# Second value tile of a local attention: 64 of its 96 rows copied from the first value tile by GpSimd instead of loaded by DMA

## The chip, the core and the metric

The kernel runs on one core of a Trainium2 chip. The metric is the device time of one execution in microseconds (us); three runs of the kernel before have a median of 644.54 us (642.48 to 645.26). The engines are TensorE (PE; its weight loads are listed as PEld), VectorE (DVE), ScalarE (ACT), GpSimd (POOL) and SyncE (SP, which here only issues DMAs). Each works through its own list of instructions in order. Waits between them are semaphores.

## What is computed

A local attention feeds a mixture of experts. Only the attention is touched.

```python
B, H, S, D = 4, 8, 768, 64            # block = 32, window = 16
k_sum = k.reshape(B, H, nb, block, D).max(axis=3)       # 24 block keys
v_sum = v.reshape(B, H, nb, block, D).mean(axis=3)      # 24 block values
scores_l = scale * q @ k.T, masked to |i - j| < 16
scores_s = scale * q @ k_sum.T + log(block)
a = softmax(concat[scores_l, scores_s])
attn = a @ concat[v, v_sum]
# then: noisy top-2 gate over 8 experts, relu(x @ w1) @ w2, weighted sum
```

For 64 queries the mask leaves at most 64 + 2*16 = 96 keys. With the 24 block keys a block of 64 queries thus has 120 keys and 120 value rows.

## The kernel before

**Tiles.** The attention goes through 24 tiles of 128 queries (4 batches of 6 tiles, all 8 heads at once). Tile t = 6*b + j is treated as two blocks of 64 queries (`blk` 0 and 1), each with its own 120 keys in `KX[t % 3]` and its own 120 value rows. The values of block 0 are `VE[b % 2][:, j]`: a tile of 128 rows loaded by `load_ve` (rows P*j to P*j+127 of the padded values `vt`), of which rows 0 to 95 are the local values; rows 96 to 119 are overwritten with the 24 block sums once these are computed. The values of block 1 are `VD[b % 2][j % 3]`: rows 0 to 23 hold the block sums, and `v_load` brings rows P*j+64 to P*j+159 of `vt` into rows 24 to 119. Each row is 8 heads of 65 floats, 520 in all (64 values and a one, which gives the softmax's denominator). Rows 64 to 95 of block 0's tile and the first 32 rows of block 1's are the same values; so are rows 0 to 31 of the next tile's `VE` and the last 32 rows of block 1's.

**Columns of the keys.** `L0 = (0, NB)` says where the 96 local keys stand among the 120: for block 0 at 0 to 95 with the block keys behind, for block 1 the block keys stand in columns 0 to 23 and the local keys behind them.

**The order of the work** is written out by hand in one loop over t from -2 to 22. Iteration t records, in this order: the normalization of tile t-1 on DVE (`norm`, L363 to L369; from the second batch on with `kx_sum(t+3)` on GpSimd inside it); the scores of tile t+2 on PE (`scores`, L318); the row maximum of tile t+2 on DVE (`smax`, L325); the transposes of tile t+1's probabilities on PE (`p_trans`, L341); the mask of tile t+3 (`mask_sums`, L308); the exponentials of tile t+2 on ACT (`sexp`, L333); `kx_local(t+3)`, two GpSimd copies of local keys into `KX` (L124); the transposes of the finished tile t-1 (`x_pe`, L378); the product of probabilities and values of tile t on PE (`av`, L354); then `v_load(t+3)`, one DMA on SP's queue (L290), and `x_out(t-2)`. Other work hangs at fractions of t in a table `todo` (`at`, `run`): key and value loads of the next batch, `v_sums` (block sums of the values on PE, copied out of PSUM, and for batch 0 copied on by six GpSimd copies, L273 and L275, for batch 1 by one, L269), `fill` (GpSimd memsets of 128x1024, L222), the steps of the gate, weight loads.

**The end of the attention.** At t = 20.2, 20.8 and 21.8 GpSimd issues three indirect DMAs (`x_gather(0, 0..2)`, recorded at L90), which gather 128 token rows each for expert 0 into the tiles `xg`. Behind the loop PE transposes two of them (`x_tr`, L835), then does `av(23)`, and then starts expert 0's first matmuls (`mm1`, L854).

**How a dependence is kept.** A copy of GpSimd that reads a value tile waits for its DMA by a semaphore of the DMA (DMAHW for SP's DMAs, DMASW for GpSimd's own); PE waits for GpSimd by a count of its finished instructions. PE, being in order, holds everything behind a matmul that waits.

## Time and profile before

| | |
|---|---|
| median of 3 runs | 644.54 us (642.48 to 645.26) |
| profiled execution, its own time | 642.6 us |
| its span, first to last instruction | 640.8 us, mean granted TensorE clock 0.997 |
| PE / DVE / ACT / POOL busy | 622.5 / 481.3 / 315.9 / 249.0 us |
| attention | roughly the first 130 us of the span |
| DMA traffic | 127.93 MB; `v_load`: 24 DMAs of 195.0 KB, `load_ve`: 24 of 260.0 KB |

The profile is of one execution. "Busy" of PE is modelled from pipelined matmuls. In a timeline row the columns are start and length in us, engine, line of the kernel, operation, output tile <- input tiles, shape, and how many were merged; the brackets tell the idle time before and what ended it. In a row of waits they are who waited for whom, us in total, how often, and the longest. "issue" is idle time for which the profile shows no semaphore.

### The profile page before, as it was taken

How to read it: one execution, taken by the hardware profiler on the slowest of the kernel's cores; microseconds unless marked ns; L12 is line 12 of the kernel's file. 1: busy time of each engine (PE TensorE's matmuls, PEld its weight loads, DVE VectorE, ACT ScalarE, POOL GpSimd, SP SyncE). 2: the span in 40 equal slices, each digit the busy share in tenths (PEclk: the TensorE clock that was granted, in tenths of full speed). 3: DMA queues.
4: the chain of work that ended last, by engine and by line, in shares of the span. 5: the costliest groups of instructions: out<-in, count | busy, mean ns of one | idle time of the engine just before them, and what ended most of it. 6: DMA issues, size and time to landing. Idle time of an engine off the chain costs nothing.

```text
span 640.8 us, 14153 instructions
## 1 busy us (share of the span) xinstructions
PE 622.5 (97%) x5295; PEld 358.8 (56%) x5295; DVE 481.3 (75%) x1039; ACT 315.9 (49%) x692; POOL 249.0 (39%) x432
## 2 busy tenths in 40 slices
PE   8999999999999999999999999999999999999995
PEld 7778777765654544555455544554554455445542
DVE  5768999889796797188868887987898679757410
ACT  4868988941253553075437534654464255425200
POOL 4442224203254324532573266336523532333041
PEclk9999999999999999999999999999999999999998
DMA  9999986788379976547886597759677767763021
GB/s 308 333 292 351 292 266 201 222 318 250 118 217 171 253 186 170 211 122 140 209 265 152 131 228 245 181 133 250 201 189 156 218 205 166 182 198 105 3 96 51
DMA packets 123708, 127.93 MB, mean 200 GB/s; under 512 B 83242, under 2 KB 86674, under 8 KB 123630
## 3 DMA queue, kind: packets, MB, share of 16 engines
q1 hardware_dynamic: 111838, 90.66, 53.3%
q0 software_dynamic: 11792, 36.27, 18.0%
q8 instruction: 44, 0.72, 0.5%
q14 instruction: 34, 0.28, 0.1%
HBM read 81.85 MB, written 25.61 MB: 168 GB/s over the span
## 4 chain that ended last, share of the span: by engine, by line
PE 82%; DVE 6%; issue 3%; DMA 3%; ACT 2%; POOL 1%; SPq 1%; POOLq 0%; DVEq 0%; ACTq 0%
PE pt L1431 29%; PE h L1359 16%; PE h L854 8%; PE pt L909 5%; PE pt L341 3%; PE pt L1359 3%; PE o L1359 3%; PE s L318 3%; PE o L354 3%; PE h L909 2%; DMA xte<-x 2%; PE pt L378 1%; PE o L246 1%; DVE y L920 1%; DVE htl L1394 1%
## 5 line engine op out<-in xcount | busy, mean ns | idle before, releaser
L90 POOL DMA_INDIRECT out_dram<-y,tb x52 | 69.3, 1333 | 169.4 <-DVE y L931 131.6
L90 POOL DMA_INDIRECT xg<-xd,tb x54 | 60.1, 1112 | 118.1 <-DVE dsc L653 32.3
L1431 PEld LDWEIGHTS <-hth 128*128 128x128 f16 x576 | 56.4, 98 | 66.7
L931 DVE SCALAR_TENSOR_TENSOR y<-pt,tb,prev 128x512 f32<-128x512 f32 x42 | 31.5, 750 | 67.4 <-PE pt L1431 49.8
L1359 PEld LDWEIGHTS <-w1h 128*128 128x128 f16 x504 | 48.9, 98 | 38.0 <-issue 4.1
L1431 PE MATMUL pt<-w2h,hth 128*128 128x512 f16 x288 | 69.0, 379 | 0.0
L1431 PE MATMUL pt<-w2h,htl 128*128 128x512 f16 x288 | 69.0, 379 | 0.0
L1431 PE MATMUL pt<-w2l,hth 128*128 128x512 f16 x288 | 69.0, 379 | 0.0
L1359 PEld LDWEIGHTS <-w1l 128*128 128x128 f16 x504 | 49.3, 98 | 34.9
L90 POOL DMA_INDIRECT prev<-out_dram,tb x45 | 52.4, 1165 | 23.7 <-issue 12.8
L333 ACT ACTIVATE p<-s,nm 128x120 f32<-128x120 f32 x192 | 51.0, 376 | 0.8
L854 PE MATMUL h<-xte,w1h 128*128 128x384 f16 (+2 forms) x248 | 48.9, 336 | 1.1 <-DMA xte<-x 1.1
L1431 PEld LDWEIGHTS <-htl 128*128 128x128 f16 x288 | 28.2, 98 | 34.0
L1348 ACT ACTIVATE w1h<-stg 128x768 f16<-128x768 f32 (+1 forms) x24 | 22.7, 944 | 37.9 <-DVE stg L1339 37.9
L1391 ACT ACTIVATE hth<-h 128x384 f16<-128x384 f32 (+4 forms) x48 | 23.8, 496 | 35.6 <-PE h L1359 35.6
L1348 ACT ACTIVATE w1l<-stg 128x768 f16<-128x768 f32 (+1 forms) x24 | 22.5, 942 | 37.2 <-DVE stg L1339 37.2
L1359 PE MATMUL h<-xte,w1h 128*128 128x384 f16 (+4 forms) x180 | 39.7, 329 | 0.7 <-DVE h L1385 0.4
L1359 PE MATMUL h<-xte,w1l 128*128 128x384 f16 (+4 forms) x180 | 39.7, 329 | 0.0
L1339 DVE TENSOR_TENSOR stg<-stg 128x256 f32<-128x256 f32 x96 | 36.2, 419 | 0.8
L854 PEld LDWEIGHTS <-w1h 128*128 128x128 f16 x256 | 24.7, 98 | 20.5 <-issue 2.2
L1312 ACT ACTIVATE x<-xt 128x512 f16<-128x512 f32 (+2 forms) x44 | 26.3, 625 | 19.6 <-issue 17.3
L1394 DVE SCALAR_TENSOR_TENSOR htl<-h,hth 128x384 f16<-128x384 f32 (+4 forms) x48 | 26.3, 562 | 11.8 <-ACT hth L1391 11.5
(301 smaller groups left out, 1292.0 us busy)
## 6 DMA issues: line engine op xcount, KB each, us to landing
stg<-in_w_dram SPq DMA_DIRECT2D x64, 512.0 KB
q<-in_qt_dram SPq DMA_DIRECT2D x24, 256.0 KB
xd<-x SPq DMA_DIRECT2D x24, 256.0 KB
out_dram<-xg SPq DMA_DIRECT2D x8, 768.0 KB
kb<-in_kt_dram SPq DMA_DIRECT2D x6, 768.0 KB
hth<-in_vt_dram SPq DMA_DIRECT2D x12, 260.0 KB
htl<-in_vt_dram SPq DMA_DIRECT2D x16, 195.0 KB
ve<-in_vt_dram SPq DMA_DIRECT2D x12, 260.0 KB
```

The lines of the kernel that those rows point to most:

```text
L90: return nc.gpsimd.indirect_dma_start(**kw)
L333: nc.scalar.activation(PE_[t][:, a, hp, :], SC[t][:, a, hp, :], AF.Exp, bias=NM[t][:, 1, a, hp:hp + 1], scale=0.125)
L854: nc.tensor.matmul(ph[:, :n], w1_of(w, wn, c, f), x[:, xo + c, c0:c1], start=(k == 0), stop=(k == 11))
L909: nc.tensor.matmul(py, hx[:, f, c * P:c * P + P], wv[:, f, :], start=st, stop=sp)
L931: nc.vector.scalar_tensor_tensor(y, py[:, :d], gw, pv[:, :d], op0=OP.mult, op1=OP.add)
L1312: nc.scalar.activation(t[:r, c:c + k], src, AF.Copy)
L1339: nc.vector.tensor_tensor(o, x, y, op=op)
L1348: nc.scalar.activation(hi, x, AF.Copy, scale=W1S)
L1359: nc.tensor.matmul(ph[:, :h], w[:, la, a, P * j:P * j + P], x[:, j, :h], start=start and k == 0, stop=k == 5, skip_group_check=True)
L1391: nc.scalar.activation(hh[:, f, t], src, AF.Relu)
L1394: nc.vector.scalar_tensor_tensor(hl[:, f, t], src, 0.0, hh[:, f, t], op0=OP.max, op1=OP.subtract)
L1431: nc.tensor.matmul(py, x, wv[:, f, :], start=st, stop=sp, skip_group_check=True)
```

## The change

Block 1's value tile gets the layout of block 0's: 96 local rows first, block sums in rows 96 to 119 (`L0 = (0, 0)`, and in `v_sums`, `v_rest` and `kx_sum` the matching places). `v_load` now brings only rows 32 to 63 of the tile (32 rows, 65 KB; for the last tile of a batch rows 32 to 95). A new function `v_copy(t)` lets GpSimd copy rows 0 to 31 from rows 64 to 95 of `VE[:, j]`, and (except in the last tile of a batch) rows 64 to 95 from rows 0 to 31 of `VE[:, j+1]`: 44 copies of 32x520 floats in all. `v_copy(0)` is recorded after the first key copies, `v_copy(t+2)` at the end of iteration t, behind `v_load(t+3)`.

```diff
--- before.py
+++ after.py
@@ -95,7 +95,7 @@
     HWD = 840
     HT = [moe.tile([P, FC, HWD], F16, name=x) for x in ("hth", "htl")]
     KB, KX = [], []
-    L0 = (0, NB)
+    L0 = (0, 0)
     for i in range(2):
         KB.append(keep.tile([P, HP, KW], F32, name=f"kb{i}"))
     for i in range(QN):
@@ -126,8 +126,7 @@
     def kx_sum(t):
         b, j = divmod(t, TS)
         if j < QN:
-            x = KX[t % QN].rearrange("p h b k -> p h (b k)")[:, :, W:W + 2 * NB]
-            (nc.gpsimd if b else nc.vector).tensor_copy(x.rearrange("p h (b n) -> p h b n", b=2),
+            (nc.gpsimd if b else nc.vector).tensor_copy(KX[t % QN][:, :, :, W:W + NB],
                                                         KM[b][:, :, None, :].to_broadcast([P, HP, 2, NB]))
 
     def q_piece(t):
@@ -256,7 +255,7 @@
             for g in range(4):
                 nc.tensor.matmul(pt[32 * g:32 * g + NB, 0:C4], ind[:, j, :], VE[b % 2][:, j, C4 * g:C4 * g + C4],
                                  start=(j == 0), stop=(j == TS - 1), skip_group_check=True)
-        x, y = VE[b % 2][W:W + NB], [z[0:NB] for z in VD[b % 2]]
+        x, y = VE[b % 2][W:W + NB], [z[W:W + NB] for z in VD[b % 2]]
         for g in range(4):
             i, o = pt[32 * g:32 * g + NB, 0:C4], slice(C4 * g, C4 * g + C4)
             if b == 3 and g % 2:
@@ -280,15 +279,23 @@
         nc.sync.dma_start(x[:, j:], x[:, 0, None, :].to_broadcast([NB, TS - j, VB]))
         if b:
             for y in VD[b % 2][b == 1:]:
-                nc.sync.dma_start(y[0:NB], x[:, 0])
+                nc.sync.dma_start(y[W:W + NB], x[:, 0])
 
     VX = {}
 
     def v_load(t):
         b, j = divmod(t, TS)
         y = VD[b % 2][j % 3].rearrange("p (h d) -> p h d", h=H)
-        nc.sync.dma_start(y[NB:NB + VR], vt[b, P * j + 64:P * j + 64 + VR])
+        n = 32 if j < TS - 1 else 64
+        nc.sync.dma_start(y[32:32 + n], vt[b, P * j + 96:P * j + 96 + n])
         VX[t] = [VE[b % 2][:, j].rearrange("p (h d) -> p h d", h=H), y]
+
+    def v_copy(t):
+        b, j = divmod(t, TS)
+        x, y = VE[b % 2], VD[b % 2][j % 3]
+        nc.gpsimd.tensor_copy(y[0:32], x[64:96, j])
+        if j < TS - 1:
+            nc.gpsimd.tensor_copy(y[64:96], x[0:32, j + 1])
 
     SC, PE_, PT, PO, X, XT = {}, {}, {}, {}, {}, {}
 
@@ -1071,6 +1078,7 @@
         if t == -1:
             q_piece(2)
             q_piece(3)
+            v_copy(0)
         run(t + 0.5)
         if t + 2 < NT:
             smax(t + 2)
@@ -1105,6 +1113,8 @@
         run(t + 0.9)
         if 0 <= t and t + 3 < NT:
             v_load(t + 3)
+        if -1 <= t and t + 2 < NT:
+            v_copy(t + 2)
         if t >= 2:
             x_out(t - 2)
 
```

On GpSimd's list, first place: tiles 1 to 4, right after the block sums of batch 0. `htl<-hth` 24x520 and `hth<-hth` 24x520 are the six copies of block sums, `htl<-hth` 32x520 the new copies, `kx_94<-kb_91` is `kx_local(4)`, the keys for the scores of tile 4. Before:

```order
L275 COPY htl<-hth 24x520 [waits DMAHW6_49,DVE_49,Pool_49]
L273 COPY hth<-hth 24x520 [waits DMAHW7_49,PE_49]
L275 COPY htl<-hth 24x520
L273 COPY hth<-hth 24x520 [waits DMAHW0_49,PE_49]
L275 COPY htl<-hth 24x520
L273 COPY hth<-hth 24x520 [waits DMAHW1_49,PE_49]
L124 COPY kx_94<-kb_91 128x4x96 [waits Activation_49,Pool_49]
L124 COPY kx_94<-kb_91 128x4x96 [waits Activation_49]
```

and now:

```order
L274 COPY htl<-hth 24x520 [waits DVE_49]
L272 COPY hth<-hth 24x520 [waits PE_49]
L274 COPY htl<-hth 24x520
L272 COPY hth<-hth 24x520 [waits DMAHW0_49,PE_49]
L274 COPY htl<-hth 24x520
L272 COPY hth<-hth 24x520 [waits DMAHW1_49,PE_49]
L296 COPY htl<-hth 32x520
L298 COPY htl<-hth 32x520
L296 COPY htl<-hth 32x520
L298 COPY htl<-hth 32x520
L124 COPY kx_94<-kb_91 128x4x96 [waits Activation_49,Pool_49]
L124 COPY kx_94<-kb_91 128x4x96 [waits Activation_49]
```

Four copies, `v_copy(1)` and `v_copy(2)`, now stand between the block sums and the keys of tile 4; `v_copy(0)` stands ahead of the block sums.

Second place: the block sums of batch 1 (`vd_102<-ve` 24x520), a memset (`xg`), and the keys of tile 8 (`kx_95`). Before:

```order
L269 COPY vd_102<-ve 24x520 [waits DMAHW6_49,DVE_49,Pool_49]
L222 MEMSET xg_165 128x1024
L130 COPY kx_95<-kmax 128x4x48 [waits PE_49,Pool_49]
L124 COPY kx_95<-kb_92 128x4x96
L124 COPY kx_95<-kb_92 128x4x96 [waits DMAHW1_49]
```

and now:

```order
L268 COPY vd_102<-ve 24x520 [waits DMAHW6_49,DVE_49,Pool_49]
L221 MEMSET xg_165 128x1024 [waits Pool_49]
L296 COPY vd_102<-ve 32x520
L298 COPY vd_102<-ve 32x520 [waits DMAHW7_49,Pool_49]
L129 COPY kx_95<-kmax 128x8x24 [waits PE_49,Pool_49]
L124 COPY kx_95<-kb_92 128x4x96
L124 COPY kx_95<-kb_92 128x4x96 [waits DMAHW1_49]
```

The two copies of `v_copy(6)` stand ahead of the three that fill the keys of tile 8.

Third place: the end of the attention, the three gathers for expert 0 (`DMA xg<-xd`). Before:

```order
L90 DMA xg_165<-xd,tb_181 128x512 [waits DMAHW3_49,DMAHW5_49,DMAHW2_49,DMAHW6_49,DMAHW0_49,DVE_49]
L768 MEMSET tl 128x16
L769 MEMSET side 64x1
L770 MEMSET side 64x1 [waits Pool_49]
L89 MEMSET spacer 1x1
L90 DMA xg_165<-xd,tb_181 128x512
L89 MEMSET spacer 1x1 [waits Pool_49]
L90 DMA xg_166<-xd,tb_181 128x512
L1163 MEMSET hth 128x8x40 [waits DMAHW7_49]
```

and now:

```order
L90 DMA xg_165<-xd,tb_181 128x512 [waits DMAHW5_49,DMAHW6_49,DMAHW2_49,DVE_49]
L775 MEMSET tl 128x16
L776 MEMSET side 64x1
L777 MEMSET side 64x1 [waits Pool_49]
L89 MEMSET spacer 1x1
L90 DMA xg_165<-xd,tb_181 128x512
L296 COPY vd_103<-ve 32x520 [waits DMASW1_49,DMASW0_49,PE_49]
L298 COPY vd_103<-ve 32x520 [waits DMAHW4_49]
L89 MEMSET spacer 1x1 [waits Pool_49]
L90 DMA xg_166<-xd,tb_181 128x512 [waits Pool_49]
L296 COPY htl<-ve 32x520 [waits DMASW2_49,PE_49]
L1173 MEMSET hth 128x8x40 [waits DMAHW7_49,Pool_49]
```

`v_copy(22)` stands between the second and the third gather, with a wait for the landing of the first two (DMASW0, DMASW1), and `v_copy(23)` behind the third, with a wait for its landing (DMASW2). No other engine's order changes; the 24 DMAs of `v_load` keep their places in SP's queue.

## The prediction

> **What bounds the kernel now.** I read the page's first part, then the busy times by stretch, then what PE waited for, then the chain of waits and the timelines at the places that the order of instructions changes.

> ```profile
> span 640.8 us, 14153 instructions
> PE 622.5 (97%) x5295; PEld 358.8 (56%) x5295; DVE 481.3 (75%) x1039; ACT 315.9 (49%) x692; POOL 249.0 (39%) x432
> ...
> 0.00:20.00 20.00, 18.05 (x343) 15.67 (x347) 11.36 (x32) 11.12 (x35) 9.49 (x39) 1.00 0.95 316
> 20.00:60.00 40.00, 37.57 (x796) 29.86 (x789) 29.16 (x73) 32.07 (x104) 15.35 (x33) 1.00 1.00 323
> 60.00:100.00 40.00, 38.72 (x804) 30.78 (x807) 37.52 (x122) 35.69 (x113) 12.40 (x21) 1.00 0.88 275
> 100.00:130.00 30.00, 27.12 (x529) 21.59 (x518) 27.14 (x109) 25.82 (x79) 9.07 (x20) 1.00 0.66 209
> ```

> The four lower rows are stretches of the attention; behind the length stand the busy times of PE, PEld, DVE, ACT and POOL, the granted clock, the DMA engines' share and GB/s. PE is busy nearly all the time, at a granted clock of 1.00; GpSimd is under half busy; the DMA engines are full (1.00) from 20 to 60 us.

> ```profile
> PE pt L341 <- issue: 2.6, 2, 1.4
> ...
> PE h L854 <- DMA xte<-x: 1.1, 1, 1.1
> PE o L354 <- issue: 0.9, 1, 0.9
> ...
> PE s L835 <- DVE xte L825: 0.3, 1, 0.3
> PE pt L854 <- ACT xte L827: 0.2, 1, 0.2
> ```

> So PE sets the end, and its few pauses in the whole execution sum to about 10 us. In the attention not one of the larger ones is a wait for a DMA: the full DMA queues do not hold PE. A change here gains little by moving bytes, and loses whatever it makes PE wait.

> **The change part by part.**

> *Bytes.* 24 DMAs of 195.0 KB become 20 of 65 KB and 4 of 130 KB: 4.68 MB become 1.82 MB. That is 2.9 of 127.93 MB. About half lies in the first 60 us, some 1.4 MB, which at 323 GB/s is 4.4 us of full queues. As PE waits for none of these loads, I count 0. The bound below: the three pauses called "issue" (2.6 + 0.9 = 3.5 us), two of which lie in the full stretch, could be made by the load on the queues and vanish; the bound above is 0.

> *Forty-four copies on GpSimd.*

> ```profile
> L273 POOL COPY hth<-hth 24x520 f32<-24x520 f32 x3 | 1.9, 619 | 0.2
> L275 POOL COPY htl<-hth 24x520 f32<-24x520 f32 x3 | 1.8, 615 | 6.2 <-issue 6.1
> ```

> These copies of 520 floats a row are the nearest rows: 615 ns where the rows move to other partitions (96 on to 0 on, L275), 619 ns where they stay, so the move is free; 32 partitions instead of 24 I take as free too, since every partition has the same 520 elements. 44 * 0.615 = 27 us on an engine with 46 us of work in the 130 us. On the average that fits. But GpSimd also makes the keys for which PE waits, in order, and what counts is what stands behind the copies.

> *First place: the keys of tile 4.*

> ```profile
> 17.54 0.61 POOL L275 COPY htl<-hth 24x520 f32<-24x520 f32 x1 [6.08 <-issue]
> ...
> 20.89 0.62 POOL L273 COPY hth<-hth 24x520 f32<-24x520 f32 x1
> 21.57 2.74 POOL L124 COPY kx<-kb 128x384 f32<-128x384 f32 x6
> ...
> 22.41 1.08 PE o L354 x32
> 23.50 0.98 PE s L318 x32
> 24.48 1.15 PE pt L341 x8
> ```

> Six copies of block sums start 0.67 us apart ((20.89 - 17.54) / 5) and end at 21.51; then come the keys of tiles 4 to 6, 0.46 us each (2.74 / 6), so tile 4's two are ready at 22.5, 1.0 us before the scores of tile 4 start on PE (23.50). Now `v_copy(1)` and `v_copy(2)` stand between. `v_copy(1)` ends at 21.57 + 0.67 + 0.62 = 22.86, and `av(1)`, which reads that tile, would start at 22.41: 0.45 us late. `v_copy(2)` ends at 21.57 + 3 * 0.67 + 0.62 = 24.2, the keys at 24.2 + 0.05 + 2 * 0.46 = 25.15; the scores' first matmuls need only the first of the two. PE thus does its scores at about 25.1 instead of 23.50: **+1.6 us**, and PE had no pause there that could take it up.

> *Second place: the keys of tile 8.*

> ```profile
> 41.59 0.61 POOL L269 COPY vd<-ve 24x520 f32<-24x520 f32 x1 [7.67 <-issue]
> 42.15 0.94 POOL L222 MEMSET xg<- 128x1024 f16 x1
> 43.15 0.34 POOL L130 COPY kx<-kmax 128x192 f32<-128x192 f32 x1
> 43.44 1.86 POOL L124 COPY kx<-kb 128x384 f32<-128x384 f32 x4
> ...
> 44.09 1.08 PE o L354 x32
> 45.17 0.86 PE s L318 x25
> ```

> The keys of tile 8 end at 43.44 + 0.93 = 44.4 and are wanted at 45.17. The two new copies ahead of them take 1.3 us: 45.7. **+0.5 us**. Further on GpSimd is 0.7 us and more ahead, as far as I followed it; at tile 20, where the step of the gate at L568 comes before, it may be late by 0 to 0.5 us. I take **0.2**.

> *Third place: the end.* This is the largest term.

> ```profile
> 117.10 1.28 POOL L90 DMA_INDIRECT xg<-xd,tb  x1 [12.51 <-DVE dsc L653]
> ...
> 119.36 0.99 POOL L90 DMA_INDIRECT xg<-xd,tb  x1 [0.51 <-issue]
> 120.34 0.09 POOL L89 MEMSET spacer<- 1x1 f32 x1
> 120.66 1.00 POOL L90 DMA_INDIRECT xg<-xd,tb  x1 [0.23 <-issue]
> ...
> DMA to landing us min/median/max: 5.0/6.1/7.2
> ...
> 125.02 0.27 PE L354 MATMUL o<-ve,pts 120*64 120x65 f32 x1
> ...
> 126.10 0.66 PE L835 MATMUL s<-ident,xg 128*128 128x128 f32 x4
> 126.67 0.63 PE L835 MATMUL pt<-ident,xg 128*128 128x128 f32 x4
> 127.23 0.27 PE L354 MATMUL s<-ve,pts 120*64 120x65 f32 x1
> ```

> Before, the three gathers go out back to back and PE meets their data only at L835, after `av(22)` (125.02). Now `v_copy(22)` waits until the first two have landed, the third gather is queued behind it, and `v_copy(23)` waits for the third's landing. So PE's last two products wait for two gathers one after the other. With landing after 5.0 to 7.2 us (the row of the gathers in this stretch; over the whole execution the median is 4.7):

> - second gather lands at 119.36 + 6.1 = 125.5 (124.4 to 126.5); `v_copy(22)` 1.3 us later: 126.8; `av(22)` starts 1.8 us late (0.7 to 2.8);
> - third gather issued at 126.9 instead of 120.66, alone on its way, so I take 5.0: 131.9; `v_copy(23)`, one copy of 0.6 us: 132.5; `av(23)`, due at 127.23, starts **5.3 us** late (4.3 to 8.6 with 5.0 or 7.2 for both).

> Of this the two small pauses behind it (L835 0.3 and L854 0.2) are taken up, since ACT and DVE finish the split of the first two gathered tiles meanwhile: **+4.8 us** (3.8 to 8.1). Everything behind is PE's work, 97% busy, so it shifts by the whole.

> *Layout.* The mask's and scores' matmuls and the row maximum keep their sizes; `kx_sum` writes the same 192 elements in eight pieces instead of four (0.35 us each on GpSimd, hidden but for the second place, where a doubling would add 0.3). I take 0.

> *VectorE beside a busier GpSimd.*

> ```profile
> L513 DVE TENSOR_TENSOR sel<-oh,pos x5: 215/224/734, 62.4 to 131.2; 128x64 f32<-128x64 f32 x5
> ...
> L514 DVE TENSOR_SCALAR wden<-p x5: 161/164/1298, 62.5 to 131.3; 128x4 f32<-128x4 f32 x5
> ...
> L751 DVE SCALAR_TENSOR_TENSOR w1l<-stg,w1h x8: 679/681/715, 74.3 to 111.2; 128x512 f16<-128x512 f32 x8
> ```

> Shortest, median and longest: L513 and L514 have outliers of 0.5 and 1.1 us, while most of DVE's operations (L751 here) do not. I found these outliers at two of the five gate steps, beside GpSimd's copies. The new copies start when `av` frees their tile, while DVE does `norm` and `smax`, which show no such outliers; I take 0 and keep up to 5 * 1.6 = 8 us of DVE time as the bound, of which PE would see what falls where DVE is as full as PE (27.14 against 27.12 us of 30 from 100 us on): two of the five steps, 3.2 us.

> [...]

> *Sum:* 1.6 + 0.5 + 0.2 + 4.8 = **+7.1 us**. The profiled execution took 642.6 us (span 640.8 and 1.8 around it): 649.7. It lies 1.9 us under the median of the three runs (644.54), from which the sum is 651.6. I predict the middle, **650.7 us**, slower by 1%.

> **The rivals.**

> *Lighter queues (not slower), 12%.* The place is the DMA queues. If the "issue" pauses and the gathers' 5.0 to 7.2 us are both made by the load on them, the pauses go (-3.5) and the gathers land sooner. With d for a landing, `av(23)` is on time if 119.36 + 2d + 2.05 is no later than 127.23: d = 2.9 us or less decides. Then 642.6 + 2.3 - 3.5 = 641.4, or 643.3 from the median. For it: DMA share 1.00 where two of the pauses lie. Against: the share is 0.66 where the gathers run, and no landing there was under 5.0.

> *VectorE held by GpSimd, 15%.* The copies meet the gate's steps, DVE becomes the bound from 100 us on: +3.2 on top of the sum, 653.9. For it the outliers; against, where the copies fall.

> *The end costs less, 8%.* The landings come near the lower end and PE's other order hides half of it: +2.3 and +2, some 647.

> **How the numbers follow.** Forecast 65%, the rivals 12, 15 and 8%. The range runs from the end with landings of 5.0 and small terms at the first places (642.6 + 0.5 + 3.3 = 646.4) to the largest ones from the median (644.5 + 2.8 + 8.1 = 655.4): 646 to 656, which takes in the second and third rivals and leaves out the first. About 0.5%, 3.2 us, can be told from no change. Slower by more: forecast and the second rival, 80%. Within: the third and most of the first, 16%. Faster by more: 4%, if more pauses go than I count.

> **What would show it.** On GpSimd a long idle time before the copies of tiles 22 and 23, ended by the gathers' landing, and the third gather some 6 us later behind the second than now. On PE a wait of 1 to 3 us before `av(22)`, one of 2 to 6 us before `av(23)`, and one of 1 to 2 us before the scores of tile 4 with GpSimd as releaser. The pauses called "issue" show the first rival, L513 and L514 the second. I am wrong if PE's last two products start without waiting for GpSimd.

## The result, and the profile after

The changed kernel takes 650.25 us (median of 13 runs, 648.59 to 653.95), the kernel before beside it 644.77 us (13 runs, 642.26 to 649.47). The ratio is 1.0092, 95% interval 1.0072 to 1.0113: slower by 5.9 us. The forecast was 650.7 us, 646 to 656, slower. The profiled execution took 649.97 us, with a span of 648.1 us. The mean granted TensorE clock is 0.990, 0.997 before.

From the page of the changed kernel:

```profile
PE 626.5 (97%) x5295; PEld 362.6 (56%) x5295; DVE 486.5 (75%) x1039; ACT 316.2 (49%) x692; POOL 279.7 (43%) x476
```

and its busy times by stretch (columns as in the prediction):

```profile
20.00:60.00 40.00, 38.27 (x818) 30.34 (x813) 30.17 (x75) 32.52 (x106) 27.06 (x50) 1.00 0.93 304
60.00:100.00 40.00, 38.38 (x788) 30.49 (x784) 38.46 (x121) 35.36 (x113) 20.76 (x34) 1.00 0.78 245
100.00:130.00 30.00, 24.64 (x462) 19.94 (x462) 26.94 (x102) 24.71 (x76) 16.18 (x28) 0.94 0.56 182
```

GpSimd is 30.7 us busier (279.7 against 249.0), the DMA engines less full (0.93 and 0.78 against 1.00 and 0.88). PE loses nothing up to 100 us. From 100 to 130 us it is busy 24.64 us instead of 27.12, and there its clock is 0.94 instead of 1.00.

The waits of PE in the changed kernel (who for whom: us, times, longest):

```profile
PE o L614 <- DVE acc L589: 2.2, 1, 2.2
PE o L361 <- POOL vd L298: 2.1, 1, 2.1
...
PE pt L348 <- issue: 1.0, 1, 1.0
PE s L325 <- POOL kx L124: 0.7, 1, 0.7
...
PE s L361 <- POOL htl L296: 0.5, 1, 0.5
```

Three waits for GpSimd stand where the prediction put waits: the keys of tile 4 (L124), `av(22)` (L298) and `av(23)` (L296). The largest, ahead of the matmul of `gate_t0` (L614), is for VectorE; before it was 0.4 us. Of the pauses called "issue" one of 1.0 us is left of three (3.5 us).

GpSimd at the end of the attention, timeline of the changed kernel:

```profile
119.18 1.28 POOL L90 DMA_INDIRECT xg<-xd,tb  x1 [6.74 <-DVE dsc L660]
...
121.43 1.00 POOL L90 DMA_INDIRECT xg<-xd,tb  x1 [0.53 <-issue]
128.09 0.61 POOL L296 COPY vd<-ve 32x520 f32<-32x520 f32 x1 [5.66 <-DMA xg<-xd,tb]
128.75 1.07 POOL L298 COPY vd<-ve 32x520 f32<-32x520 f32 x1
...
130.12 1.15 POOL L90 DMA_INDIRECT xg<-xd,tb  x1
133.68 0.61 POOL L296 COPY htl<-ve 32x520 f32<-32x520 f32 x1 [2.41 <-DMA xg<-xd,tb]
```

and, from the view of line L90 (the gathers) in this stretch, the time from issue to landing:

```profile
DMA to landing us min/median/max: 3.7/5.1/6.5
```

This row holds two landings, 3.7 us for the first gather and 6.5 for the second; the third one's is not told. The row of the kernel before that the prediction quotes (5.0 to 7.2 us) holds two as well. `v_copy(22)` idles 5.66 us until the second gather has landed, the third gather goes out at 130.12, 8.7 us behind the second (1.3 before), and `v_copy(23)` waits 2.41 us for it.

Where the time came from shows best from fixed points, counted from PE's first scores matmul (tile 0), since the start itself varies (9.3 to 10.3 us among the profiles here, with and without copies). "22, 23 loaded" (e10) and "layout" (e3) are two of the kernels below.

| us from the scores of tile 0 to | before | changed | 22, 23 loaded | layout |
|---|---|---|---|---|
| scores of tile 4 | 14.10 | 14.86 | 14.90 | 14.07 |
| scores of tile 5 | 19.46 | 19.29 | 19.32 | 19.44 |
| scores of tile 8 | 35.77 | 35.10 | 35.08 | 35.52 |
| scores of tile 20 | 92.85 | 92.70 | 93.15 | 92.80 |
| scores of tile 22 | 102.82 | 104.92 | 104.51 | 102.79 |
| `av(23)` | 117.90 | 123.28 | 120.51 | 118.81 |
| end of the span | 631.47 | 637.94 | 635.05 | 632.92 |

The changed kernel is level up to tile 20, loses 2.1 us up to tile 22 and 3.3 more up to `av(23)`, and 1.1 behind it. Beside "22, 23 loaded" it loses 2.8 us up to `av(23)` and 2.9 up to the end.

### The profile page after: what moved, and what is told of

Read it like the earlier page. It is cut to its first block, busy times and chain, and to the rows that moved or that the text cites. A ratio compares the mean times of both kernels' runs of the same rounds, so it can differ in the third digit from the quotient of the medians.

```text
span 648.1 us, 14209 instructions
## 1 busy us (share of the span) xinstructions
PE 626.5 (97%) x5295; PEld 362.6 (56%) x5295; DVE 486.5 (75%) x1039; ACT 316.2 (49%) x692; POOL 279.7 (43%) x476
## 4 chain that ended last, share of the span: by engine, by line
PE 81%; DVE 8%; DMA 3%; issue 3%; POOL 2%; ACT 2%; SPq 1%; POOLq 0%; DVEq 0%; ACTq 0%
PE pt L1441 29%; PE h L1369 16%; PE h L861 8%; PE pt L916 7%; PE pt L1369 3%; PE o L1369 3%; DMA xg<-xd,tb 2%; PE h L916 2%; PE pt L348 2%; PE s L325 2%; PE o L361 2%; PE o L245 1%; DVE nm L332 1%; DVE y L927 1%; PE pt L385 1%
## 5 line engine op out<-in xcount | busy, mean ns | idle before, releaser
L90 POOL DMA_INDIRECT out_dram<-y,tb x52 | 69.4, 1334 | 167.2 <-DVE y L938 128.8
L90 POOL DMA_INDIRECT xg<-xd,tb x54 | 60.5, 1121 | 112.1 <-DVE rh L1397 30.7
L90 POOL DMA_INDIRECT prev<-out_dram,tb x45 | 52.2, 1160 | 24.5 <-issue 12.7
L1358 ACT ACTIVATE w1l<-stg 128x768 f16<-128x768 f32 (+1 forms) x24 | 22.5, 942 | 37.3 <-DVE stg L1349 37.3
```

The costliest lines, as they stand in the source:

```text
L90: return nc.gpsimd.indirect_dma_start(**kw)
L1358: nc.scalar.activation(hi, x, AF.Copy, scale=W1S)
```

## The experiments

Five timed rounds each; ratios are to the kernel before on the same chip, with their 95% intervals. The diffs are against the changed kernel.

| kernel | median us | ratio |
|---|---|---|
| changed, again (e9) | 651.67 | 1.0100 (1.0072 to 1.0128) |
| tiles 22, 23 loaded (e1) | 647.31 | 1.0015 (0.9989 to 1.0041) |
| the same again (e10) | 647.04 | 1.0016 (0.9995 to 1.0036) |
| copies 22, 23 ahead of the gathers (e2) | 648.83 | 1.0039 (1.0013 to 1.0065) |
| only tile 23 loaded (e11) | 650.67 | 1.0075 (1.0049 to 1.0101) |
| layout alone (e3) | 646.10 | 0.9979 (0.9950 to 1.0008) |
| short loads, no copies (e4) | 643.19 | 0.9957 (0.9932 to 0.9982) |
| tiles 18 to 23 loaded (e5) | 645.69 | 1.0007 (0.9982 to 1.0032) |
| tiles 0 to 2 and 18 to 23 loaded (e6) | 645.73 | 0.9986 (0.9961 to 1.0011) |
| memsets in place of copies (e7) | 645.43 | 0.9998 (0.9980 to 1.0016) |
| layout and 8 copies nobody reads (e8) | 649.52 | 1.0053 (1.0031 to 1.0075) |
| PE kept busy ahead of `gate_t0` (e12) | 653.04 | 1.0111 (1.0090 to 1.0132) |

### The end: tiles 22 and 23

Both tiles by DMA, without their copies:

```diff
     def v_load(t):
...
-        n = 32 if j < TS - 1 else 64
-        nc.sync.dma_start(y[32:32 + n], vt[b, P * j + 96:P * j + 96 + n])
+        if t >= 22:
+            nc.sync.dma_start(y[0:VR], vt[b, P * j + 64:P * j + 64 + VR])
+        else:
+            n = 32 if j < TS - 1 else 64
+            nc.sync.dma_start(y[32:32 + n], vt[b, P * j + 96:P * j + 96 + n])
...
     def v_copy(t):
+        if t >= 22:
+            return
```

> The changed kernel, but tiles 22 and 23 get all 96 rows by DMA and no copy. The theory (the copies' waits for the gathers make most of the loss, +4.8 us in the prediction, +6.2 us at av(23) in the trace): the waits of PE for GpSimd before av(22) and av(23) are gone, the third gather goes out within 2 us of the second, and the time is 4.8 us under the changed kernel's 650.3, 645.5 us (644 to 647), ratio to the kernel before 1.001. The rival (VectorE, held by the copies of tiles 18 to 21, makes most of the loss; its lag shows as the 2.2 us pause of PE before L614): the time stays at 649 us or above, ratio 1.006 or more, and that pause is still there.

Measured: ratio 1.0015 instead of 1.0092, 0.77% or 5.0 us, but the medians are only 2.9 us apart (647.31 and 650.25, not taken side by side). The waits for GpSimd before both products are gone; the pause ahead of `gate_t0`'s matmul is still 2.18 us. As 2.9 and 5.0 tell the size of the term badly, both kernels were run once more on one chip.

> The changed kernel once more, to stand beside the next three on one chip. Ratio 1.009 (1.006 to 1.011) in every theory; PE again waits for GpSimd ahead of the scores of tile 4, av(22) and av(23), and about 2.2 us ahead of gate_t0's matmul.

> e1_end_loaded once more (tiles 22 and 23 by DMA, without copies), beside the changed kernel on the same chip: its medians were 2.9 us under the changed kernel's, its ratio to the kernel before 5.0 us. Theory A (the prediction's term for the end, 4.8 us, is right): 4.8 us under e9_change_again, 3.8 or more. Rival B (the term was too large, since the profiled executions differ by only 3.1 us at av(23) and 2.7 us in span): 3 us, under 3.8.

Measured: 651.67 and 647.04, 4.6 us apart; by the ratios (1.0100 and 1.0016) 5.4 us, above the 3.8 of theory A. But the six runs of the changed kernel reach from 650.06 to 654.48 us, the intervals of the two ratios leave some 2 us either way, and the two profiled executions differ by only 3.2 us from the scores of tile 0 to the end, 2.7 of it at `av(23)`. So the end costs 3 to 6 us: the forecast 4.8 lies in this range, and rival B's 3 us is not excluded. The waits of PE between 10 and 136 us with tiles 22 and 23 loaded again (e10):

```profile
PE o L619 <- DVE acc L594: 2.2, 1, 2.2
PE o L366 <- DVE lt L418: 1.5, 1, 1.5
...
PE s L330 <- POOL kx L124: 0.7, 1, 0.7
```

No wait for a value tile is left among them; the first one (L619 is `gate_t0`'s matmul in this kernel) has nothing to do with the end. The second, 1.5 us in `av(21)`, is only 0.5 us long in the changed kernel. So the changed kernel comes to `av(22)` 1.1 us sooner, and of its wait of 2.11 us there 1.3 are a loss.

The copies kept, but placed ahead of the gathers:

```diff
-        at((20.2, 20.8, 21.8)[c], x_gather, 0, c, P * BATCH[GROUP0][0])
+        at((20.8, 20.8, 21.8)[c], x_gather, 0, c, P * BATCH[GROUP0][0])
...
         run(t)
+        if t == NT - 4:
+            v_copy(t + 2)
+            v_copy(t + 3)
         run(t + 0.8)
...
-        if -1 <= t and t + 2 < NT:
+        if -1 <= t < NT - 4:
             v_copy(t + 2)
```

> The changed kernel with the same DMAs and copies, but the copies of tiles 22 and 23 are recorded ahead of the three gathers (behind av(20)) and the first gather goes with the second (20.8 instead of 20.2). The theory (it is the place behind the gathers that costs): as when they are loaded, 645.5 us (644 to 647), ratio 1.001; the copies do not wait for xg. The rival (VectorE held by copies): no gain, since the four copies only move to where VectorE has its gate step at about 117 us: 649 us or more.

Measured: 648.83, ratio 1.0039. GpSimd's timeline of this kernel:

```profile
115.35 0.64 POOL L296 COPY vd<-ve 32x520 f32<-32x520 f32 x1 [3.16 <-PE o L361]
...
119.78 0.61 POOL L296 COPY htl<-ve 32x520 f32<-32x520 f32 x1 [3.12 <-PE o L361]
...
121.57 1.28 POOL L90 DMA_INDIRECT xg<-xd,tb  x1 [0.80 <-DVE pos L504]
...
123.16 1.00 POOL L90 DMA_INDIRECT xg<-xd,tb  x1 [0.21 <-issue]
...
124.46 1.00 POOL L90 DMA_INDIRECT xg<-xd,tb  x1 [0.21 <-issue]
```

The copies now wait for PE alone, for the tile to come free, and the gathers go out back to back: the place behind the gathers is what makes the copies wait. But only 0.53% of the 0.77% come back, though the intervals overlap. PE pauses 2.2 us ahead of `gate_t0` as before, and again 2.2 us in `av(21)` (1.5 in e10), a pause that the profile calls "issue" and whose cause stays open; behind both the clock is low (0.57 in 112 to 116 us, 0.78 in 124 to 128).

Only tile 23 by DMA, `v_copy(22)` left between the gathers (the first diff with `t == 23`):

> The changed kernel with only tile 23 by DMA and without its copy; v_copy(22) still stands behind the first two gathers and ahead of the third. Theory A (two waits one after the other, av(22) +1.8 and av(23) +5.3 in the prediction, of which the second contains the first): the wait ahead of av(22) stays at 2 us, the one ahead of av(23) is gone, av(23) comes 4.3 us after av(22) or sooner instead of 6.0, and the time is between the changed kernel and the one with both tiles loaded: 1.5 to 3 us under e9_change_again. Rival B (the queued third gather is what costs, whoever reads tile 23): PE waits as long at the transposes of the gathered tiles, and the time stays within 1 us of e9_change_again.

Measured: 650.67, 1.0 us under the changed kernel beside it, ratios 0.25% apart, less than their intervals. That misses the 1.5 to 3 us of theory A and is what rival B said of the time; but PE waits for no gather at the transposes, as B would have it. PE at the end (L366 is `av`, L847 the transposes of the gathered tiles; the profile is of one of the longer executions, 652.67 us):

```profile
130.93 0.37 PE L366 MATMUL o<-vd,pts 120*64 120x65 f32 x1 [2.80 <-POOL vd L303]
...
132.86 1.12 PE L847 MATMUL s<-ident,xg 128*128 128x128 f32 x4
```

and in the changed kernel:

```profile
129.88 0.27 PE L361 MATMUL o<-vd,pts 120*64 120x65 f32 x1 [2.11 <-POOL vd L298]
...
131.54 1.12 PE L842 MATMUL s<-ident,xg 128*128 128x128 f32 x4
132.45 1.06 PE L842 MATMUL pt<-ident,xg 128*128 128x128 f32 x4
...
134.34 0.27 PE L361 MATMUL s<-htl,pts 120*64 120x65 f32 x1 [0.50 <-POOL htl L296]
```

Without the second copy `av(23)` waits for nothing and follows 3.8 us behind `av(22)`, as theory A said, yet with it it follows 4.5 us behind, and only 0.50 us of that is a wait. So there is little to gain: the time between is PE's own work at a low clock (0.78 and 0.80 in 128 to 136 us in the changed kernel, 0.71 and 0.50 here). The wait of `v_copy(22)` for two gathers, with the third gather behind it, makes most of the end's cost: this kernel, which keeps it, takes 3.6 us more than the one without both copies (1.0075 and 1.0016, intervals apart), and the second copy adds 1.0 us, which the noise can hide.

### Layout and bytes

All rows by DMA and no copies (`v_load` always brings 96 rows, `v_copy` returns at once):

> Only the layout of the change: block sums in rows 96 to 119 and keys at column 0 for both blocks, all 24 tiles with 96 rows by DMA, no copy by GpSimd. The theory (layout counts 0): 644.8 us, ratio 1.000 (0.998 to 1.002). The rival (the layout costs, by kx_sum in eight pieces or by where scores and mask write): 646.5 us or more, ratio 1.003 or more.

Measured: 0.9979, with 1 in the interval. The layout costs nothing that shows. Its three "issue" pauses are there (2.5 + 0.9 us).

The short loads from the fourth tile of each buffer pair on, no copies:

```diff
+        if b < 2 and j < 3:
+            nc.sync.dma_start(y[0:VR], vt[b, P * j + 64:P * j + 64 + VR])
+        else:
             n = 32 if j < TS - 1 else 64
             nc.sync.dma_start(y[32:32 + n], vt[b, P * j + 96:P * j + 96 + n])
```

> The layout of the change and its short DMAs (32 or 64 rows instead of 96) from the fourth tile of each buffer pair on, but no copies: the rows that GpSimd would bring keep what an earlier tile left, so this part of the values is left out. The theory (fewer bytes count 0): 644.8 us, ratio 1.000 (0.997 to 1.002). The rival (lighter queues: the pauses of PE called issue, 3.5 us, come from the load of the queues and vanish): 641.3 us, ratio 0.9945.

Measured: 0.9957, which is 2.8 us under the kernel before, below the theory's range and nearer the rival's 0.9945. But the layout alone is at 0.9979, and of the 0.22% (1.4 us) between the two the intervals leave open whether it is nothing. Fewer bytes are worth something from 0 to 3 us. Whether it is the rival's way stays open. "Issue" pauses of PE stand in this profile too, 4.4 us in all (0.9, 1.1 and 2.4), the one in `av(2)` among them; but the one near 84 us (1.2 us in the kernel before and with the layout alone) is gone, and the profile is of the longest of the twelve executions (649.09 us).

### VectorE beside the copies

Tiles 18 to 23 by DMA (the first diff with `t >= 18`):

> As e1_end_loaded, and tiles 18 to 21 get all 96 rows by DMA too: copies for tiles 0 to 17 only. Theory A (the copies of these tiles lengthen VectorE's small operations of the gate between 100 and 112 us, and PE waits for them): the pause of PE ahead of the matmul of gate_t0, 2.18 us in e1_end_loaded and 0.44 in e3_layout, is back at about 0.45; from the scores of tile 18 to those of tile 22 19.5 us pass (21.7 in e1_end_loaded, 19.5 in e3_layout); the time is 1.5 to 2.5 us under that of e1_end_loaded, ratio about 0.998. Rival B (the lag comes from the short DMAs or from copies further ahead): the pause stays at 2.2 us and the ratio at 1.0015.

The waits of PE in this kernel, between 10 and 136 us:

```profile
PE pt L353 <- issue: 1.6, 2, 1.0
...
PE s L330 <- POOL kx L124: 0.7, 1, 0.7
...
PE o L619 <- DVE acc L594: 0.4, 1, 0.4
```

Measured: the pause ahead of `gate_t0` is 0.4 us, and 20.2 us pass from the scores of tile 18 to those of tile 22 (21.7 in e1, 19.5 in the layout alone). Theory A by the trace; the times alone (1.0007 and 1.0015) do not tell 1.5 us apart. What happens is read from VectorE's timeline ahead of that matmul, with the copies (e10):

```profile
106.85 0.58 DVE L552 TENSOR_TENSOR wa<-wa,p 128x4 f32<-128x4 f32 x1
...
107.68 0.47 DVE L561 SCALAR_TENSOR_TENSOR val<-wa,val 128x8 f16<-128x8 f32 x1
108.05 1.59 DVE L544 TENSOR_TENSOR hth<-iotar,rf 128x512 f16<-128x512 f16 x2
109.57 0.51 DVE L609 TENSOR_TENSOR oc<-iotac,qf 128x56 f16<-128x56 f16 x1
110.11 0.83 DVE L612 TENSOR_TENSOR hth<-oc,val 128x84 f16<-128x84 f16 x2
```

and without (layout alone):

```profile
107.31 0.16 DVE L552 TENSOR_TENSOR wa<-wa,p 128x4 f32<-128x4 f32 x1
...
107.71 0.18 DVE L561 SCALAR_TENSOR_TENSOR val<-wa,val 128x8 f16<-128x8 f32 x1
107.80 1.28 DVE L544 TENSOR_TENSOR hth<-iotar,rf 128x512 f16<-128x512 f16 x2
109.00 0.21 DVE L609 TENSOR_TENSOR oc<-iotac,qf 128x56 f16<-128x56 f16 x1
109.24 0.41 DVE L612 TENSOR_TENSOR hth<-oc,val 128x84 f16<-128x84 f16 x2
```

The same five rows are longer by 0.42 + 0.29 + 0.31 + 0.30 + 0.42 = 1.74 us, and the pause is longer by 2.19 - 0.44 = 1.75 us. VectorE works without a pause there, so each of these holds goes through to PE. GpSimd's rows beside them are new copies for L552, L561 and L612 (1.13 us) and key copies (L124) for L544 and L609 (0.61 us): without the new copies ahead of them the key copies are done by then (at 105.4 us with the layout alone).

Eight copies that nobody reads, in the places of the copies of tiles 18 to 21 (against the layout alone):

```diff
     def v_load(t):
...
+        for i in range(2 if 19 <= t < 23 else 0):
+            z = VD[b % 2][j % 3][0:32, 0:4 * P].rearrange("p (a b) -> p a b", a=4)
+            nc.gpsimd.tensor_copy(z, ident[0:32, None, :].to_broadcast([32, 4, P]))
         nc.sync.dma_start(y[0:VR], vt[b, P * j + 64:P * j + 64 + VR])
```

> e3_layout (all rows by DMA) plus eight copies of 32x512 from a constant by GpSimd, two ahead of each of the loads of tiles 19 to 22, into rows that the load writes afterwards: they stand where the changed kernel has the copies of tiles 18 to 21, but nothing reads them. Theory A (what delays PE at gate_t0 is the copies themselves beside VectorE): VectorE's L525 to L612 between 100 and 112 us are longer by 1.5 us or more in sum, the pause ahead of gate_t0's matmul grows from 0.44 to 1.5 or more, time 1.5 us over e3_layout's, ratio 1.000 to 1.001. Rival B (it is the data's way: the copied tile is late for av): nothing changes, ratio 0.998.

Measured: the pause ahead of `gate_t0` is 1.9 us, as theory A said, and 21.3 us pass from the scores of tile 18 to those of tile 22. So copies alone, with the key copies that they push, make the lag, with no data behind them. The time does not fit either theory: 4.8 us over the layout alone (0.74%). In the profile 2.7 us of it are there at the scores of tile 16 (74.5 against 71.8 us from tile 0), ahead of any added copy. Where they come from stays open, and the time of this kernel is not used.

A memset in place of each copy, to see whether it makes VectorE's operations longer as a copy does (the pause ahead of `gate_t0` would then stay at 2.2 us) or not (0.44, as with the layout alone):

```diff
-        nc.gpsimd.tensor_copy(y[0:32], x[64:96, j])
+        nc.gpsimd.memset(y[0:32], 0.0)
         if j < TS - 1:
-            nc.gpsimd.tensor_copy(y[64:96], x[0:32, j + 1])
+            nc.gpsimd.memset(y[64:96], 0.0)
```

> The changed kernel with a GpSimd memset to zero in the place of each of the 44 copies, same rows and same destination: rows 0 to 31 and most of rows 64 to 95 of the second value tiles are zero, so this part of the values is left out. [...]

Measured: 0.9998. The waits for the gathers are gone, so it is the copies' reading of `ve` that brings them. The pause ahead of `gate_t0` is 1.5 us, between the two. The rows ahead of it show why:

```profile
106.98 1.25 POOL L124 COPY kx<-kb 128x384 f32<-128x384 f32 x2
107.33 0.46 DVE L547 TENSOR_TENSOR wa<-wa,p 128x4 f32<-128x4 f32 x1
...
109.54 0.96 POOL L124 COPY kx<-kb 128x384 f32<-128x384 f32 x2
109.59 0.52 DVE L604 TENSOR_TENSOR oc<-iotac,qf 128x56 f16<-128x56 f16 x1
```

What holds VectorE here are the key copies, which read SBUF and which the memsets have pushed to this place. Four operations beside them (L547, L555, L604, L607) are longer by 0.30 + 0.25 + 0.31 + 0.19 = 1.05 us than with the layout alone, and the pause is 1.08 us longer (1.52 against 0.44); the operations beside a memset alone (L556, L539) keep their length (0.18 us, and 1.28 for the two of L539). So all but 0.03 us of the longer pause comes from beside the key copies. Elsewhere in the attention of this run, where only a memset ran beside them, some of VectorE's small operations with one input (TENSOR_SCALAR, CAST, COPY, a reduction) were up to 0.25 us longer than their shortest, while the nine TENSOR_TENSOR with two inputs in SBUF (one of L544's kind among them) stayed within 0.01 us of theirs. Where only a new copy ran beside such a TENSOR_TENSOR, six of eight lost 0.3 to 0.44 us (e9).

Which of the two is longer went with which started first. The changed kernel, two places with L758 (L751 of the kernel before, 0.68 us alone), first beside a new copy, then beside the second key copy:

```profile
79.05 0.68 DVE L758 SCALAR_TENSOR_TENSOR w1l<-stg,w1h 128x512 f16<-128x512 f32 x1
79.06 1.16 POOL L298 COPY htl<-hth 32x520 f32<-32x520 f32 x1
...
89.69 0.95 POOL L124 COPY kx<-kb 128x384 f32<-128x384 f32 x2
90.25 0.95 DVE L758 SCALAR_TENSOR_TENSOR w1l<-stg,w1h 128x512 f16<-128x512 f32 x1
```

At 79.05 VectorE is first, by 0.01 us, and the copy takes 1.16 us instead of 0.61; at 90.15 (the second of the two merged copies) GpSimd is first, and L758 takes 0.95 us. The same was seen in each of the 16 cases of a TENSOR_TENSOR with two inputs in SBUF beside new copies only, in the two profiles of the changed kernel (the first one and e9): the ten that began behind the copy lost 0.3 to 0.44 us, the six that began ahead of it (by 0.02 to 0.12 us) nothing.

### The first place

Tiles 0 to 2 by DMA as well (the first diff with `t < 3 or t >= 18`):

> As e5_gate_loaded, and tiles 0 to 2 get all 96 rows by DMA too: copies for tiles 3 to 17 only. Theory A (the keys of tile 4 are late only because of the copies ahead of them): PE waits no longer for GpSimd ahead of the scores of tile 4, and these start 14.1 us after those of tile 0 (14.9 in the changed kernel); but the pause of 0.9 us called issue in av(2), which lies in the same place in the kernel before and is gone where PE waited just ahead of it, comes back, so the gain is only 0.3 us, ratio 0.997 to 0.998. Rival B (the issue pause stays away since it came from the load on the DMA queues): 1.2 us gained, ratio 0.996.

Measured: 0.9986, level with the kernel before and with e5. The scores of tile 4 start 14.07 us after those of tile 0, without a wait; the pause called "issue" in `av(2)` is back with 0.81 us; and the scores of tile 5 start after 19.29 us, to the hundredth as in the changed kernel. Theory A: the wait for the keys of tile 4 stands in the shadow of a pause that comes a little later anyway. No version that computes the whole beat the kernel before by more than the measurement tells.

### The clock behind PE's pause

```diff
     def mask_sums(t):
...
-        for blk in range(2):
+        for blk in range(2) if t != 22 else (0, 1) * 6:
```

> The changed kernel, with the four mask matmuls of tile 22 done six times over (20 more of 0.09 us, the same result): they stand where PE waits 2.2 us ahead of gate_t0's matmul. Theory A (the low granted clock behind that pause, 0.64 in 112 to 116 us, comes from the pause of PE): with PE busy the clock is 1.00 there, from gate_t0's first matmul to the scores of tile 22 pass 1.9 us as in the kernel before (2.7 in the changed kernel), and the time is 0.9 us under e9_change_again or the same, since the end waits for the gathers anyway. Rival B (the low clock has another cause): the clock in 112 to 116 us stays under 0.8.

Stretches of the changed kernel, the granted clock is the third number from the right:

```profile
112.00:116.00 4.00, 3.63 (x64) 3.34 (x68) 3.86 (x23) 3.09 (x12) 0.44 (x2) 0.64 0.00 0
128.00:132.00 4.00, 2.12 (x32) 2.00 (x33) 2.65 (x6) 1.27 (x4) 2.92 (x4) 0.78 0.15 52
132.00:136.00 4.00, 3.50 (x49) 2.96 (x48) 2.54 (x7) 1.71 (x3) 1.31 (x4) 0.80 0.33 117
```

and with PE kept busy:

```profile
112.00:116.00 4.00, 3.24 (x80) 2.85 (x80) 3.90 (x21) 3.09 (x11) 0.82 (x3) 1.00 0.05 15
...
132.00:136.00 4.00, 4.00 (x42) 3.38 (x40) 2.31 (x5) 1.71 (x3) 1.10 (x4) 0.50 0.38 121
```

Measured: the clock is 1.00 in 112 to 116 us, and from `gate_t0`'s first matmul to the scores of tile 22 1.86 us pass (2.71 in the changed kernel). Theory A on the clock. The time is not better, 653.04 against 651.67: PE comes to `av(22)` sooner and waits there 3.0 us instead of 2.1, since the gathers set the moment, and behind that longer pause the clock is 0.50.

## Why the prediction was right, and where it was not

The sign, the size of the whole and the place of the largest term were right. Two other terms were wrong, by about the same amount in opposite directions; that they cancel is luck.

- **The end, +4.8 us: right in its mechanism, its size known only to 3 to 6 us.** By time it is 2.9 us (e1), 4.6 (e9 and e10) or 5.0 to 5.4 (ratios), by the traces about 3. The second gather landed 6.5 us after its issue (6.1 taken), `av(22)` waited 2.11 us (1.8), and `v_copy(23)` began 3.6 us after the third gather's issue (5.0 taken for the landing alone). `av(23)` came 5.4 us later than in the kernel before, as the step "5.3 us late" said, but 2.1 us of this stood already at tile 22 and have nothing to do with the gathers. The second wait is 0.50 us; the rest of the end is the first wait and PE's slower work behind it, and the latter the prediction did not have. Two of its sums are slightly off: with landings of 5.0 us the step gives 4.2 us, not 4.3, and the range's lower end takes 3.3 us for the end where the text gives 3.8; neither changes the outcome.
- **The first place, +1.6 us: mis-sized, and not paid.** PE waited 0.72 us for the keys and its scores took 0.43 us longer, as the second key copy came late: about 1.2 us. The step that failed is "PE had no pause there that could take it up": the 0.9 us pause called "issue" in `av(2)`, quoted in that same prediction as one of three, came just behind and vanished. At tile 5 nothing of it is left, and e6 gives both back together.
- **The second place, +0.5, and tile 20, +0.2: nothing.** The keys of tile 8 were ready at 44.84 us, their scores began at 45.26. GpSimd had begun the block sums ahead of them at 40.56 us, 1.0 sooner than before. What made it sooner is not shown.
- **VectorE, 0: wrong.** From the scores of tile 21 to those of tile 22 the changed kernel takes 7.35 us instead of 4.77: 1.74 by VectorE's longer operations, the rest by the clock behind the pause (0.64 from 112 to 116 us), which was 1.00 there in e1 and e10. The second rival had the mechanism, in other rows than it named: L513 and L514 (L520 and L521 in the changed kernel) have outliers of 0.64 and 0.47 us, no more than before. Its price of 3.2 us was near the 2.6 found in the trace. In the times less is seen: without the end's copies, and with the holds in place, the kernel is 1.0 us over the kernel before (e1, interval -0.7 to 2.6). The step that failed was the argument that the copies fall beside `norm` and `smax`: ahead of `gate_t0` they fall beside L544 to L612. The reading of L751 as an operation without outliers failed too: in the kernel before a GpSimd operation ran beside only two of its eight, and in the changed kernel it mostly starts first, and then GpSimd's copy is the longer one (0.98 to 1.16 us instead of 0.61).
- **Bytes, 0 (bound -3.5), layout, 0: not refuted.** The layout's interval holds 0. The loads without copies gained 2.8 us on the kernel before (interval 1.2 to 4.4) and 1.4 on the layout, the latter within the noise. Two "issue" pauses did go in the changed kernel. The one in `av(2)` stayed in e4 with the shorter loads, so there it is PE's wait ahead that takes it up; the one near 84 us is gone in e4 too, so the shorter loads may be what removes it, which is not shown.
- **Copies, 27 us:** GpSimd became 30.7 us busier. A copy alone takes 0.61 us as forecast; five of the 44 took 0.98 to 1.16, all beside L758.

Counted together: the 2.3 us forecast for the first places did not come, the 2.6 us at VectorE were not counted, and the end came in the range forecast for it or a little under. The middle of the forecast is met so well (650.7 and 650.25) because these errors cancel.

## What to carry to other kernels

What an idle engine's work costs was set here by what stood behind it in its list: the 33 copies of tiles 0 to 17 (some 20 us of GpSimd's time) cost nothing that the time shows (e5), and three copies of two tiles that stood behind a gather cost 3 to 6 us. Before a wait is added up, look for a pause of the same engine shortly behind it: here the 0.72 us of waiting for the keys of tile 4 took up the pause in `av(2)`, and without the copies of tiles 0 to 2 the pause was back with 0.81 us (e6). Ahead of `gate_t0`, where VectorE had no slack, GpSimd's copies were not beside its work but in it (1.74 us), and which operations became longer can be read row by row from a timeline with and without them.

## What the runs showed of the hardware

```profile
7.33:113.14 105.81, 99.69 (x2074) 79.44 (x2072) 88.97 (x237) 86.25 (x274) 64.46 (x109) 1.00 0.82 266
109.73:113.14 3.41, 1.23 (x18) 0.73 (x16) 3.31 (x9) 1.43 (x4) 2.53 (x6) 1.00 0.06 21
113.14:116.56 3.42, 3.42 (x64) 3.29 (x64) 3.21 (x23) 3.11 (x11) 0.00 (x0) 0.50 0.10 23
116.56:130.21 13.65, 10.64 (x196) 8.34 (x193) 11.10 (x50) 11.67 (x36) 4.50 (x10) 1.00 0.70 224
126.80:130.21 3.41, 1.25 (x16) 0.94 (x18) 3.34 (x18) 2.21 (x5) 1.86 (x4) 1.00 0.49 185
130.21:133.62 3.41, 3.41 (x37) 2.96 (x32) 1.51 (x5) 0.67 (x2) 1.06 (x1) 0.50 0.20 65
```

and two of e1, whose pause lasts from 109.91 to 112.09 us:

```profile
107.70:111.11 3.41, 2.21 (x44) 1.49 (x36) 3.31 (x10) 2.02 (x7) 3.22 (x5) 1.00 0.31 101
111.11:114.53 3.42, 2.44 (x67) 2.21 (x71) 3.35 (x13) 2.51 (x9) 0.99 (x3) 1.00 0.00 1
```

The clock's record in the changed kernel runs from 7.33 to 642.21 us at 1.00 but for two stretches at 0.50, of 3.413 us each; the stretches at 1.00 are 31, 4 and 149 times as long. In the kernel before the clock is 1.00 from 5.27 to 636.73 us, 185 times 3.413 us. Cut into steps of this length, the two profiles have four steps with 2.17 to 3.31 us without PE work (two at the pauses of the changed kernel, the last of each profile, in which PE's work ends), and behind each the clock is 0.50; no other step up to there has more than 1.37 us, and behind all of them it is 1.00. In the changed kernel the whole pause at `gate_t0` (110.19 to 112.37 us) lies in one step (PE idle 2.18 us of 3.41); in e1 the border at 111.11 us cuts it into 1.2 and 1.0 us, and the clock stays. That the place of a pause against these steps decides is the author's estimate from these cases: no run moved the pause alone. In the changed kernel the low stretch costs 0.9 us from `gate_t0` to the scores (2.71 against 1.86 in e12).
- **A pause called "issue" of 0.8 to 0.95 us went where PE had waited 0.7 us ahead of it.** It stood in `av(2)` with 0.8 to 0.95 us in the kernel before, in e3, e4 and e6, and is gone in all profiles in which PE waited 0.7 us for the keys of tile 4 some 4 us earlier. In the kernel before, e3, e4 and e7 it ends at the same time, 18.95 to 18.97 us from the scores of tile 0, and in e7, where PE had waited 0.3 us, 0.21 us of it are left, as if it waited for something that comes at a set time. What that would be stays open; in e8 the pause is missing without such a wait.
- **How much longer VectorE's operations were beside GpSimd's.** Summed over the attention (10 to 135 us), each VectorE operation's length over the shortest of its kind in all profiles: 4.9 us before, 5.7 with the layout alone, 10.0 with the 44 copies, 7.9 with those of tiles 0 to 17 (e5), 10.2 with the memsets (e7), where other operations are longer and the key copies are pushed as well. Of it, the 1.74 us ahead of `gate_t0`, where VectorE had no slack, show in a pause of PE.
